# Weight loads moved from SyncE's queue to GpSimd's, one buffer of P for each step parity, and a new order, in a transformer kernel on one core

## The chip, the core and the metric

The kernel runs on one core of one Trainium2 chip. Its engines are TensorE (matmuls; PE in the profile, PEld for its weight loads), VectorE (DVE), ScalarE (ACT), GpSimd (POOL) and SyncE (SP, which issues DMAs only). SyncE, ScalarE and GpSimd can each issue DMAs, each in the order of its own queue. The metric is the device time of one launch in microseconds, lower is better.

## The reference

Two layers with the same weights run one after the other: attention over segments of 32 tokens with a recurrent memory of 8 tokens, then a gated feed-forward block (F = 4608), both with layer norm and a residual, on x of 2048 x 576.

```python
for s in range(n_seg):                       # 64 segments, one after the other
    h = concat([mem, xs], axis=1)            # 8 memory rows + 32 rows of x
    q, k, v = h @ Wq, h @ Wk, h @ Wv         # 32 heads of 128
    p = softmax(where(mask, q @ k.T * scale, -1e9))
    o = (p @ v) @ Wo
    mem = o[:, :M]                           # goes into the next segment
    outs.append(o[:, M:])
...
x = x + A(layernorm(x), mem0, ...)
x = x + (silu(h @ w1) * (h @ w3)) @ w2       # h = layernorm(x)
x = x + A(layernorm(x), mem0, ...)
x = x + (silu(h @ w1) * (h @ w3)) @ w2
```

## The kernel before

A step is one segment of layer 0 together with the segment of layer 1 that is eight behind it (LAG = 8), 72 steps in all; where both run, their 40 rows each are handled side by side. The attention weights stay in SBUF. The feed-forward weights don't fit beside them, so they are loaded again for each group of 128 tokens: in 18 pairs of 128 columns of F, 304 pair loads over the kernel. A pair needs five DMAs: two of 256 KB and two of 32 KB into W13 (its nine row chunks of w1 and w3; a 256 KB one has 512 rows of 512 bytes, a 32 KB one 64), and one of 288 KB into W2C (256 rows of 1152 bytes). W13 and W2C have two buffers each. The profile lists W13 as W.

The softmax of a step runs in four groups of eight heads (NG = 4). VectorE adds the mask and takes the maximum, ScalarE the exponential, VectorE the sum, and multiplies P into PB in the columns that the next matmul needs (`sm_pb`: the columns differ between steps of even and odd parity, `role(t)`). A DMA transposition on SyncE's queue (`ptd`, 224 of them) brings PB to PTS, or TensorE transposes it (`ptr`) where one layer runs alone. PB has two buffers, used by even and odd groups. Since a step writes other columns than the one before, the first two groups of each step wait for a memset of their buffer, which is GpSimd's work (`pb_zero`, 142 of them).

The order of all work comes from a planner. `make_nodes` (line 236 on) makes a node for each piece of work, with an engine, an assumed duration and the slots of buffers that it takes and frees. `plan` then takes TensorE's pieces in the order of the string ORDER, one letter a piece, and puts the work of the other engines into their queues as their assumed durations let it start. An assumed duration is no measurement; it only decides the order in a queue. ORDER is FIRST (16 steps), then FOUR (4 steps) eleven times, then LAST. The letters that matter here:

- Q, q: q and k (full rows, then the last 64 rows of the contraction in row mode); S: scores; T: transposition of P on TensorE; P: P times V; O, o: the product with Wo
- V, v, X, x, G, g: v
- F, f: the two halves of the product with w1 and w3 (full rows, then the last 64 in row mode); W, w: the product with w2, for layer 0 and 1
- m, a, b, p, n: transpositions for mem0, layer norms and residuals

TensorE runs in several array modes (full, col, row, c32, oct, quad), and `plan` keeps to one mode as long as the pieces allow it.

Layer norm (`ln_nodes`) is a chain over engines: statistics on VectorE, the power -1/2 on GpSimd (`ln_pow`, 64 of them), normalising into XN on VectorE, transposition on TensorE.

SyncE's queue holds, in one order, the loads of attention weights at the start, all feed-forward loads (1520 DMAs for the pair loads), the transpositions of P, the XN loads of x and at the end the weights of the last group. GpSimd's queue holds the memsets of PB, the powers, 16 loads of x into XR, and the stores. Eight semaphores are used in turn by the DMAs of each kind of queue, so a DMA also waits until the one eight before it has landed.

Of the kernel before, what the change touches and what calls it, by code (L numbers as in the profile page):

```python
# [13 lines left out]
P = 128  # L14
R64 = 64
D = 576
# [183 lines left out]
def ewh(*ns):  # L200
# [5 lines left out]
    "maqqQqQSqTQQQSqQqqSQTQqSXxVvPPTTOOPoPOooOoQqqqqQQSQVvSqqQQQTQSqqXTSPOPTPOOTooPoxOoQQqqqqQSQvVqSQqQQQSqqTPSTOPoOT"  # L206
    "PTOPooOoaQqqQQSQqqVvSqQQQqqqTSQPxTSOPXOToToPPOOooQqqqpQQSVvqqQQnQSFfqqQTQSPfqFSOTFPfWoTOPFTOPoofOoFfqqQQWSFQQqqf"
    "vVqQSTFqfQWQQSqfqFPFTSXfPWTOPOxoTFoPOOffooFVqqvQQWQSQqqfFQqqfFSQTWSPQqfqFQFSTOfPWoTOPFTOPfaOoooFfqqQQvqqSQQWSfVF"
    "qQqQWQTQPqSqTOPbSOxxXTXTPooPOOooQpQQqqqqQSnQSFfqFfQvqVSfFWQqqQfPSFPOOooFfPWOFPofOoFQqqfqQWQSqqqQQQSFSGfgqQQqgfFP"
    "GSWPGfggfFFGOPoOOPWOoooFFffqqQQWSqqQQFvSqfVqQQfFSWqQQqfPPSFFOOPWoOffFPoaoOoWQqqqqQQbSQQQqqSGSgqQQqgPGSOPGggGoPOO"  # L210
    "PooOoQqqqppQQQqvVSSnnQFfqqQQQfqqSFFSPfPwOOWoFPoffFOwPWOooFqqffQQwFWQQqqFSSFffqqQQQQqqwWSSgfGFPGgggGPGOoPOOPWOooo"
    "wFqfqqQQQQSffqqFFSQQwvqVWSFQqqffFQWPwSFffPOPOOowooWFPFOoafQQqqqWSQqqqQQQSwSbQqQgqGSggGPGPOGoPgOPOOooo"
)
FOUR = (
    "QqqqppQvVSQQnnQFqfqFSfqqQQFfqQSWPwPSFffOOowFPWoOPFOooFqfqfQQwQQqqgSWGSFqqfQQQPwQSWFqffqFSGgggGPGPOOwooOPWOooFFqq"
    "ffQQQQSwVvqqfFSQQqqWPFSFfqqfQQwOSWPFFoffPOOWPwOoooFfqqQQqqaSQQqWSQQqqqQQSbwSggGGPGPOggoGPOPOOooo"
)
LAST = (
    "QqqppQQSQqqqvVSQQnqqnQSFPqffQOoSPFOFPwWOFPfooOofQQQqqqfFSwWQQFfqqfFSwWqqQQSGqffgFQFPGgWSwPFggfGOOPoGowPOOooFvfqq"
    "VQQQQSWqqFSFqqffQQQQqqSPwWSFfPOOoWwFffPFPOOooowQWQfqqqFSFfqqQQQWSqqqQQSQbvVVSPwXvxPOPOoOPooOoQQppVqqqQQSqvqnQSnQ"  # L220
    "qffFFQTSqqQTPwFfSPWTOOPFffTFooOPWwOooFffqvVQWFQQqqqQSwSQQfqqFSTFfqqQQWTPwSPFOTOffoPTFoPOOWoowxvXVqqQQFSQqfqqQQSF"
    "QQqqqfQTwPSTSWOPFOffTFPToWoPOwOooFqqfvQQQSQqqfVwWSFFfQqqQTWqSPQQqTOSPbOxooTXPTwPOOooQQpqqqQSqQVvnSqqQQqQSQFfqTFP"
    "STfOPoTOwPTFPOOooofVvqqQQQqqSQQSFfqqFQQSTwqqQTFPffSPOTOwxXooPTFPOOffooFQQqqqqQSQFSfvVqqQQQTqqSQwTPfSOFPFTOwTooPf"
    "POfOooFvVQQqwQqqqSQqqQSQfFTSqQqQfPTSPOOooFTTPPfOOoopwfFFnFwffFFwffFFwwffFfFwFfFwffFfFwFfFwffFFwffFFwffFw"
# [11 lines left out]
def make_nodes(em, nseg, pools, o=Opt, dma_bw=230e3, load_bw=400e3):  # L236
# [125 lines left out]
    def step(t):  # L362
# [17 lines left out]
        zdep = [pts_of[t - 1, k] for k in (NG - 2, NG - 1)] if t else []  # L380
        for g in range(NG):
# [88 lines left out]
    def job(j):  # L470
# [36 lines left out]
        for at, pp in enumerate([npp - 1] + list(range(npp - 1)) if last else range(split, npp)):  # L507
# [33 lines left out]
            for (bi, g) in ents:  # L541
# [3 lines left out]
                if last and at == npp - 1:  # L545
                    xn = Slot("xn")
                    for h in (0, 1):
                        e_ = node("DVE", dve(288), em.fin_add(g, h, xr[g], xn, b[h]), deps=[d], prio=prio + o.w2, acq=[xn], rel=[b[h]], name="W2a")
                        node("SWD", 1.0, em.store_half(g, h, xn), deps=[e_], prio=s0 + LAG - 4.2, lat=2.0, name="store")
# [21 lines left out]
    def x_res(g):  # L571

        xr_ld[g] = node("SWD", 1.0, em.load_x(g, xr[g]), deps=reads_ht[4 * g + 1][:1], prio=4 * g + 1.5, acq=[xr[g]], name="ldx", lat=4.0)
# [30 lines left out]
class Emitter:  # L604
# [122 lines left out]
    def load_w13(self, pr, w13):  # L727
        def f(n):
            fa = pr * 2 * P
            W = self.T.W13[:, w13.i]  # L730
            for kind, wd in ((0, self.a.w1), (1, self.a.w3)):
                self.dma(W[:, 4 * kind:4 * kind + 4], wd[0:4 * P, fa:fa + 2 * P].rearrange("(c p) f -> p c f", p=P))
            for kind, wd in ((0, self.a.w1), (1, self.a.w3)):
                self.dma(W[kind * R64:(kind + 1) * R64, 8], wd[4 * P:D, fa:fa + 2 * P])
        return f

    def load_w2(self, pr, w2):
        fa = pr * 2 * P
        return lambda n: self.dma(self.T.W2C[:, w2.i], self.a.w2[fa:fa + 2 * P, :].rearrange("(b p) d -> p b d", p=P))
# [306 lines left out]
    def pb_zero(self, pb):  # L1046
        return lambda n: self.ch("POOL", self.nc.gpsimd.memset(self.pbt(pb), 0.0))  # L1047
# [345 lines left out]
```

## Time and profile before

| | us |
|---|---|
| median of 3 runs | 2644.6 |
| lowest, highest | 2642.23, 2646.21 |
| profiled execution, whole time | 2638.71 |
| its span, first to last instruction | 2636.9 |

The profile is one execution. Its page gives for each engine the busy time; a matmul's end is modelled, so gaps shorter than about a matmul's own time (0.2 us) don't show as idle. A row such as "1058.00 0.45 PE ... x8" in an order of time has the start in us from the span's start, the time from the first start to the last end, and how many instructions were merged; "[1.86 <-ACT HT L630]" is the idle time before it and what ended it. "busy us, mean ns" stand in the groups; "572/572/722" is the shortest, median and longest duration in ns. L627, L630 and L633 are the helpers for TensorE, ScalarE and VectorE, L636 and L642 those for DMAs of SyncE and GpSimd, L1047 is the memset of PB, L1050 the transposition.

### The profile page before, as it was taken

How to read it: one execution, taken by the hardware profiler on the slowest of the kernel's cores; microseconds unless marked ns; L12 is line 12 of the kernel's file. 1: busy time of each engine (PE TensorE's matmuls, PEld its weight loads, DVE VectorE, ACT ScalarE, POOL GpSimd, SP SyncE). 2: the span in 40 equal slices, each digit the busy share in tenths (PEclk: the TensorE clock that was granted, in tenths of full speed). 3: DMA queues.
4: the chain of work that ended last, by engine and by line, in shares of the span. 5: the costliest groups of instructions: out<-in, count | busy, mean ns of one | idle time of the engine just before them, and what ended most of it. 6: DMA issues, size and time to landing. Idle time of an engine off the chain costs nothing.

```text
span 2636.9 us, 134690 instructions
## 1 busy us (share of the span) xinstructions
PE 2574.1 (98%) x60031; PEld 2222.3 (84%) x60031; DVE 2004.5 (76%) x5137; ACT 1264.2 (48%) x3745; POOL 196.7 (7%) x253
## 2 busy tenths in 40 slices
PE   5999999999999999999999999999999999999998
PEld 4788888889888888888888888888888888888886
DVE  4787777887778678777877777787777777777876
ACT  2655553444445454444545444454545445454552
POOL 1100000000000010000001001000100001010000
PEclk9999999999999999999999999999999999999999
DMA  9065755575464656546454654655465464545357
GB/s 324 4 174 135 190 104 147 130 148 139 126 147 115 139 127 155 136 131 151 113 140 116 159 140 128 155 110 139 114 156 143 132 159 94 139 122 146 106 156 247
DMA packets 683207, 371.56 MB, mean 141 GB/s; under 512 B 233753, under 2 KB 672801, under 8 KB 681985
## 3 DMA queue, kind: packets, MB, share of 16 engines
q1 hardware_dynamic: 678944, 355.00, 53.2%
q8 instruction: 469, 7.68, 1.2%
q0 software_dynamic: 3024, 6.93, 0.9%
q10 hardware_dynamic: 656, 1.02, 0.2%
q14 instruction: 114, 0.93, 0.1%
HBM read 306.72 MB, written 2.36 MB: 117 GB/s over the span
## 4 chain that ended last, share of the span: by engine, by line
PE 91%; DVE 4%; DMA 3%; issue 1%; ACT 1%; ACTq 0%; DVEq 0%; SPq 0%
PE bank L627 91%; DMA PTS<-PB 2%; DVE HTT L633 1%; DVE PB L633 1%; DVE STAT L633 1%; DMA WV<-in_A_Wv_dram 0%; DVE SME L633 0%; DMA W<-in_A_Wk_dram 0%; DVE V L633 0%; DVE QKT L633 0%; DMA W2C<-in_B_w_dram 0%; DVE XR L633 0%; ACT HTT L630 0%; ACT HT L630 0%; DVE LNS L633 0%
## 5 line engine op out<-in xcount | busy, mean ns | idle before, releaser
L627 PEld LDWEIGHTS <-W 128*128 128x128 bf16 (+2 forms) x32920 | 1261.8, 101 | 119.8 <-issue 67.8
L627 PE MATMUL bank<-HT,W 128*128 128x80 bf16 (+3 forms) x23040 | 795.2, 197 | 21.3 <-ACT HT L630 8.2
L627 PE MATMUL bank<-XTB,W 128*64 128x256 bf16 (+5 forms) x9880 | 658.4, 264 | 2.1 <-issue 1.3
L630 ACT ACTIVATE QKT<-bank 128x256 bf16<-128x256 f32 (+4 forms) x1676 | 385.1, 309 | 302.9 <-PE bank L627 296.5
L627 PE MATMUL bank<-OT,WO 128*128 128x80 bf16 (+3 forms) x11520 | 411.6, 198 | 2.5 <-issue 1.9
L627 PEld LDWEIGHTS <-WO 128*128 128x128 bf16 (+1 forms) x11520 | 383.2, 102 | 29.9 <-issue 16.3
L630 ACT ACTIVATE V<-bank 64x512 bf16<-64x512 f32 (+1 forms) x603 | 338.0, 584 | 137.4 <-PE bank L627 131.4
L627 PE MATMUL bank<-WV,HT 128*32 128x512 bf16 (+4 forms) x3576 | 363.5, 384 | 0.3 <-issue 0.2
L627 PE MATMUL bank<-W2C,HTT 128*64 128x288 bf16 (+1 forms) x3440 | 323.8, 287 | 0.5 <-DMA W2C<-in_B_w_dram 0.5
L630 ACT ACTIVATE HTT<-bank 128x512 bf16<-128x512 f32 (+1 forms) x322 | 172.6, 551 | 300.1 <-PE bank L627 299.1
L633 DVE TENSOR_REDUCE STAT<-SME 104x8 f32<-104x320 f32 (+1 forms) x576 | 274.9, 477 | 28.2 <-ACT SME L630 21.2
L633 DVE TENSOR_TENSOR PB<-SME,STAT 40x128 bf16<-40x128 f32 (+4 forms) x912 | 274.8, 335 | 9.3 <-DMA PTS<-PB 0.5
L627 PEld LDWEIGHTS <-HT 128*32 128x32 bf16 (+4 forms) x3576 | 149.2, 99 | 147.7 <-issue 37.8
L633 DVE SCALAR_TENSOR_TENSOR HTT<-HTT,bank 128x512 bf16<-128x512 bf16 (+1 forms) x322 | 201.0, 624 | 94.4 <-ACT HTT L630 91.6
L627 PEld LDWEIGHTS <-HTT 128*64 128x64 bf16 (+1 forms) x3512 | 233.1, 106 | 31.2 <-DVE HTT L633 4.1
L1047 POOL MEMSET PB<- 128x1024 bf16 x142 | 135.0, 952 | 1657.0 <-DMA PTS<-PB 1114.3
L633 DVE SCALAR_TENSOR_TENSOR XR<-bank,XR 128x288 f32<-128x288 f32 x574 | 240.0, 447 | 20.3 <-PE bank L627 17.2
L630 ACT ACTIVATE OT<-bank 128x320 bf16<-128x320 f32 (+1 forms) x383 | 144.4, 404 | 214.5 <-PE bank L627 185.3
L630 ACT ACTIVATE SME<-SME 104x320 f32<-104x320 f32 (+1 forms) x288 | 135.5, 470 | 194.3 <-DVE SME L633 192.4
L633 DVE TENSOR_TENSOR HTT<-HTT,bank 128x512 bf16<-128x512 bf16 (+1 forms) x322 | 203.3, 631 | 28.5 <-PE bank L627 1.4
L633 DVE CAST V<-bank 64x512 bf16<-64x512 f32 (+1 forms) x261 | 178.9, 686 | 40.1 <-PE bank L627 34.9
L633 DVE TENSOR_TENSOR SME<-bank,maskb 104x320 f32<-104x320 f32 (+1 forms) x288 | 138.5, 482 | 53.8 <-PE bank L627 50.1
(59 smaller groups left out, 1383.5 us busy)
## 6 DMA issues: line engine op xcount, KB each, us to landing
W<-in_B_w_dram SPq DMA_DIRECT2D x608, 256.0 KB, 3.6
W2C<-in_B_w_dram SPq DMA_DIRECT2D x304, 288.0 KB, 3.4
W<-in_B_w_dram SPq DMA_DIRECT2D x608, 32.0 KB, 3.4
W<-in_B_w_dram SPq DMA_DIRECT2D x8, 1024.0 KB, 12.6
W<-in_A_Wq_dram SPq DMA_DIRECT2D x9, 512.0 KB, 9.9
WO<-in_A_Wo_dram SPq DMA_DIRECT2D x4, 1152.0 KB, 19.1
XR<-in_A_x_dram POOLq DMA_DIRECT2D x16, 288.0 KB, 3.1
WV<-in_B_w_dram SPq DMA_DIRECT2D x4, 1152.0 KB, 7.5
```

What stands on the lines that cost most here:

```text
L627: self.ch("PE", self.nc.tensor.matmul(out, lhsT=lhsT, rhs=rhs, start=start, stop=stop, skip_group_check=True, **k))
L630: self.ch("ACT", self.nc.scalar.activation(*a, **k))
L633: self.ch("DVE", getattr(self.nc.vector, fn_)(*a, **k))
L1047: return lambda n: self.ch("POOL", self.nc.gpsimd.memset(self.pbt(pb), 0.0))
```

## The change

Three things are changed together. All pair loads (W13, W2C) go to GpSimd's queue, and the planner has new assumed durations for that queue. PB's buffer is chosen by the parity of the step instead of by that of the group, so a buffer always has the same columns written, and it is cleared only where the kernel goes from one layer to two or back: four memsets in all, on VectorE. And the strings of ORDER are new.

```diff
 FOUR = (
-    "QqqqppQvVSQQnnQFqfqFSfqqQQFfqqQSWPwPSFffOOowFPWoOPFOooFqfqfQQwQQqqgSWGSFqqfQQQPwQSWFqffqFSGgggGPGPOOwooOPWOooFFqq"
-    "ffQQQQSwVvqqfFSQQqqWPFSFfqqfQQwOSWPFFoffPOOWPwOoooFfqqQQqqaSQQqWSQQqqqQQSbwSggGGPGPOggoGPOPOOooo"
+    "QqqqppQVvSQQnnQqfFSFqqfQQQSqqfFwPWSOFffPFoPOOWwPFOoooFfqqQQQQqqSWwGSFfgqqQQwPQQSWFqfqfFGSgggGPGOPOwoOPWOooFoFqq"
+    "ffQQQQSwvVfqqFSQQqqWPFSFqffqQQWOSwPoFFPffOOWPwOoooFqfqQQqqaSQWQQqSQqqqQQSbwSGggGPGPOggGPoOOPooOo"
 )
...
-        zdep = [pts_of[t - 1, k] for k in (NG - 2, NG - 1)] if t else []
...
-            pb = Slot(f"pb{g % 2}")
-            if g < 2 and t:
-                zero = [node("POOL", 0.95, em.pb_zero(pb), deps=zdep[g:g + 1], prio=pf, acq=[pb], name="pbz")]
+            pb = Slot(f"pb{e}")
+            if g == 0 and t > 1 and both(t) != both(t - 2):
+                zero = [node("DVE", 0.65, em.pb_zero(pb), deps=[pts_of[t - 2, NG - 1]], prio=pf - 2.0, acq=[pb], name="pbz")]
...
-            node("SWD", 1.0, em.store(g, xn), deps=[c], prio=s0 + LAG - 4.2, rel=[xn], lat=3.0, name="store")
+            node("POOL", 0.6, em.store(g, xn), deps=[c], prio=s0 + LAG - 4.2, rel=[xn], lat=3.0, name="store")
...
-                    ld = [node("DMA", kb(1152, 256) / dma_bw, em.load_w13(pr_, w13), prio=prio - 1, acq=[w13], lat=2.5, name="W13")]
-                    lds.append(node("DMA", kb(256, 576) / dma_bw, em.load_w2(pr_, w2), prio=prio - 0.99, acq=[w2], lat=2.4, name="W2l"))
+                    ld = [node("POOL", 2.25, em.load_w13(pr_, w13), prio=prio - 1, acq=[w13], lat=3.0, name="W13")]
+                    lds.append(node("POOL", 0.75, em.load_w2(pr_, w2), prio=prio - 0.99, acq=[w2], lat=2.8, name="W2l"))
...
             for kind, wd in ((0, self.a.w1), (1, self.a.w3)):
-                self.dma(W[:, 4 * kind:4 * kind + 4], wd[0:4 * P, fa:fa + 2 * P].rearrange("(c p) f -> p c f", p=P))
+                self.swdma(W[:, 4 * kind:4 * kind + 4], wd[0:4 * P, fa:fa + 2 * P].rearrange("(c p) f -> p c f", p=P))
             for kind, wd in ((0, self.a.w1), (1, self.a.w3)):
-                self.dma(W[kind * R64:(kind + 1) * R64, 8], wd[4 * P:D, fa:fa + 2 * P])
+                self.swdma(W[kind * R64:(kind + 1) * R64, 8], wd[4 * P:D, fa:fa + 2 * P])
...
-        return lambda n: self.dma(self.T.W2C[:, w2.i], self.a.w2[fa:fa + 2 * P, :].rearrange("(b p) d -> p b d", p=P))
+        return lambda n: self.swdma(self.T.W2C[:, w2.i], self.a.w2[fa:fa + 2 * P, :].rearrange("(b p) d -> p b d", p=P))
...
     def pb_zero(self, pb):
-        return lambda n: self.ch("POOL", self.nc.gpsimd.memset(self.pbt(pb), 0.0))
+        return lambda n: self.v("memset", self.pbt(pb), 0.0)
```

FIRST and LAST are new in the same way. The other lines that the diff touches give loads of XR and the last stores the same new assumed durations; the DMAs themselves stay where they were. In the changed program GpSimd's queue begins, after its constants, with the ten DMAs of the first two pairs, then the power of the first layer norm; SyncE's has after the start-up weights only the XN loads, the transpositions and the last group's weights.

More of the change, by code (lines that the diff above doesn't have):

```diff
@@ L205 @@
 FIRST = (
[L206 to L210, printed above, removed]
@@ L213 @@
+    "qfFQTWqqSPQQTOPSbOxXTXPTxooPOOooQpQqqqqQSQnQQfqSFFvqfVSQFfqqQWPfSFPOFOfWPooFOPfoOoFQfqqqQQSqqqQQWQgfSFGSfqQWFPQq"
+    "gGgSFPGffgFGOPOoWPOOoooFFqqffQQWSqqQQFvSqfVQQqfFSWqQQqfPPSFOOWPoofFOFoPfaOoWQQqqqqQSQQbQSqqGSggqGQQqPPSOGGgOPgoO"
+    "ooPOoQqqppQQQSqqvVnSnQQFfqqqQQPfqSFFSPfWOOwoFffPFOWPwOooFoFffqqQQWwQQSfqqFSFfqqQWQQQqqSwSfggGFPGGPOwggGPoOPOOooo"
+    "FfqqQQQWSfqqFQQQSwFvqqfVWSFQffqqFQWaPSPwOOFffooFPwPOOWooFfqqQQqqWSQqqQQSwQbQQqqSGSggGPGPOGggOPoOPooOo"
 )
 FOUR = (
-    "QqqqppQvVSQQnnQFqfqFSfqqQQFfqQSWPwPSFffOOowFPWoOPFOooFqfqfQQwQQqqgSWGSFqqfQQQPwQSWFqffqFSGgggGPGPOOwooOPWOooFFqq"
@@ L221 @@
[L221 to L224, printed above, removed]
+    "QqqppQQSQqqqvVSQQqqnnQfSFPfqQOSoFPFOPWwOFPfooOofQQQfqqqFSQWwQFfqqfFSGWwqgfQFSqQQPFgfqGSWwOPoFggfGGPOPOOooowWvVfq"
@@ new lines @@
+    "qFQQQQqqSFSFqqffQQQQqqSwPWSFPfOOooFPWwffFPOOowoWQQFqqfFSfqqQQqWSvQQqqQSVQbqPVPSwOXvOPoxoOPoOoQQppvqqVqqQSQQqSnnQ"
+    "qqfFFTSQQPqfTOfPSFOwWTFTPooffPFOOWwooFvqfqVQQFSQWQqqqfQwSTQqqfQSFPqfFTQPWTwSPOFOffFToOWPwOxoooXVvqqQQFQqqfSQQSqq"
+    "QFqfqQwTQSPTSWPOFOffTFToPowOPWOooFqfqvQQQSQqfqVwWSFFfqqQQTWqSQPQqTOSPbOxooTXPTwPOOooQQpqqqQSqQvVnSQqQqTFSQqfqQFP"
+    "STOfPoTOwPTFPOOooofVvqqQQQqqSQFSQqqfqQQFSTwPQqffTFSPOOTwXxoPTFoPOOffooFQQqqqqQQSFfSVvQQqqqQqSTQwTPSFFfPOOTwToPof"
+    "POOooFfqvVqQQQQSqqwfqqQSFQQSTqqQfTSPPOOoofTFPTFPOOoowpfFnwFffFFwffFFwwfFffFwFfFwffFfFwFffFwFfFwffFFwffFw"
@@ L548, in job @@
                         e_ = node("DVE", dve(288), em.fin_add(g, h, xr[g], xn, b[h]), deps=[d], prio=prio + o.w2, acq=[xn], rel=[b[h]], name="W2a")
-                        node("SWD", 1.0, em.store_half(g, h, xn), deps=[e_], prio=s0 + LAG - 4.2, lat=2.0, name="store")
+                        node("POOL", 0.6, em.store_half(g, h, xn), deps=[e_], prio=s0 + LAG - 4.2, lat=2.0, name="store")
                     return
@@ L571, in x_res @@
     def x_res(g):
-        xr_ld[g] = node("SWD", 1.0, em.load_x(g, xr[g]), deps=reads_ht[4 * g + 1][:1], prio=4 * g + 1.5, acq=[xr[g]], name="ldx", lat=4.0)
+        xr_ld[g] = node("POOL", 0.6, em.load_x(g, xr[g]), deps=reads_ht[4 * g + 1][:1], prio=4 * g + 1.5, acq=[xr[g]], name="ldx", lat=4.0)
     x_in(0)
```

8 lines of the change are left out of this document (4 added, 4 removed).

## The prediction

> **What bounds the kernel now.** I read the head of the page, then the busy times by stage, then TensorE's own waits, and last the order of time at the start and in one repeated stretch.
>
> ```profile
> span 2636.9 us, 134690 instructions
> ```
>
> ```profile
> core 0: us, PE busy (x) PEld busy (x) DVE busy (x) ACT busy (x) POOL busy (x), PEclk, DMA share, GB/s
> 0.00:60.00 60.00, 30.72 (x727) 23.27 (x729) 28.07 (x68) 15.15 (x39) 8.20 (x20) 0.94 1.00 350
> 60.00:640.00 580.00, 567.35 (x14296) 487.44 (x14293) 449.16 (x1189) 291.94 (x866) 43.93 (x54) 0.99 0.54 129
> 974.43:2196.62 1222.19, 1217.70 (x27266) 1061.25 (x27264) 936.10 (x2385) 590.74 (x1769) 89.60 (x112) 1.00 0.55 135
> 2196.62:2636.90 440.28, 424.82 (x10299) 360.97 (x10295) 333.70 (x840) 201.80 (x574) 30.55 (x37) 1.00 0.54 148
> ```
>
> These are busy times by stage. The first 60 us are loading (DMA share 1.00, 350 GB/s) and TensorE idles 29.3 us of them. From 60 to 640 it idles 12.7 us and after 2196.62 another 15.5 us. In between, in eight of the eleven repetitions of FOUR (from one of its XR loads to the eighth after it, 1222.19/8 = 152.8 us each), it idles 4.5 us in all, 0.6 us a repetition. So TensorE is the bound, and visible waits after the start come to some 33 us, 1.2% of the span. That is the most that a change of waits could bring, apart from gaps too short to show; what it can lose has no such limit.
>
> ```profile
> PE bank L627 <- ACT HT L630: 8.2, 20, 1.9
> PE bank L627 <- DMA W<-in_A_Wk_dram: 6.4, 4, 3.2
> PE bank L627 <- DMA PTS<-PB: 5.0, 11, 1.4
> PE bank L627 <- DMA W2C<-in_B_w_dram: 0.5, 1, 0.5
> ```
>
> This is the view of TensorE's waits (total, times, longest). The transpositions of P, which the change frees from SyncE's loads, cost it 5.0 us in all. For the feed-forward weights it waited 0.5 us, once: today they are in time.
>
> **What is taken away.** POOL loses the 142 clearings of PB. They lay on an engine that was mostly idle.
>
> ```profile
> L1047 POOL MEMSET PB<- x142: 951/951/970, 52.9 to 2559.4; 128x1024 bf16 x142
> L642 POOL DMA_DIRECT2D XR<-in_A_x_dram x16: 572/572/722, 54.7 to 2348.2; - x16
> ```
>
> 142 x 0.951 = 135 us of POOL, of which VectorE or TensorE waited for none: worth 0. Four clearings come to VectorE in their place, each about one such memset, under 1 us: 4 us on an engine with 936.10 of 1222.19 busy, hidden by its idle 23%. Without that cover they would cost 4 us at most.
>
> **The start.** 608 loads of 256 KB, 608 of 32 KB and 304 of W2C go to POOL, five for a pair of feed-forward blocks. In the new order of POOL's queue the first ten (two pairs) stand ahead of the first layer norm's power and need no buffer to come free. In the old one SyncE issued them behind every start-up weight, from 47.17 on.
>
> ```profile
> 1.38 0.84 ACTq L639 DMA_DIRECT2D XN<-in_A_x_dram  x1
> 5.57 0.30 POOL L1347 MEMSET maskb<- 8x40 bf16 x2
> 10.27 0.82 DVE L633 BATCH_NORM_STATS2 LNS<-XN 128x6 f32<-128x288 bf16 x2 [1.82 <-DMA XN<-in_A_x_dram]
> 11.68 0.56 POOL L796 TENSOR_TENSOR LNS<-LNS,mhalf 128x1 f32<-128x1 f32 x1 [5.81 <-DVE LNS L633]
> 15.34 0.66 PE L627 MATMUL bank<-HT,W 64*128 64x40 bf16 x19 [1.86 <-ACT HT L630]
> 23.37 2.44 PE L627 MATMUL bank<-HT,W 128*128 128x40 bf16 x65 [3.16 <-DMA W<-in_A_Wk_dram]
> 47.17 6.44 SPq L636 DMA_DIRECT2D W<-in_B_w_dram  x4
> ```
>
> This is the order of time. POOL is free at 5.9 us, and until 23.37 TensorE waits for the first half of Wq and Wk. Two pairs are 2 x (2 x 256 + 2 x 32 + 288) = 1728 KB, 1.77 MB, and at 350 GB/s that is 5.1 us of a bus already full. XN, small and on ACT's queue, shows that another queue's transfer is mixed with SyncE's rather than put behind it: issued at 1.38 it had landed by 10.27, long before SyncE's queue was done. So between 0 us (all served after the weights) and 5.1 us (all served ahead of them) comes on the path up to 23.37. From there the path is TensorE's own, and no later row can hide it. I take 3.5, since the ten start 6 us after the weights did and are mixed with them for the 17 us that are left. The power at 11.68 now stands behind loads nine and ten, which wait until loads one and two have landed (eight semaphores in turn). With XN's 8.9 us from issue to use that is 5.9 + 8.9 = 14.8 or more. The matmuls follow the power by 15.34 - 11.68 = 3.7 us, so a power up to 23 us is hidden by the wait for Wk, then near 27. Past that each microsecond costs one.
>
> **The turn-round of a weight buffer.** This decides the steady part. There are two buffers, so a pair's loads start when its last reader is done and have to land before the pair after next.
>
> ```profile
> W<-in_B_w_dram SPq DMA_DIRECT2D x608, 256.0 KB, 3.6
> W2C<-in_B_w_dram SPq DMA_DIRECT2D x304, 288.0 KB, 3.4
> W<-in_B_w_dram SPq DMA_DIRECT2D x608, 32.0 KB, 3.4
> XR<-in_A_x_dram POOLq DMA_DIRECT2D x16, 288.0 KB, 3.1
> PTS<-PB SPq DMA_TRANSPOSE x224, 3.3
> ```
>
> ```profile
> 1058.00 0.45 PE L627 MATMUL bank<-PTS,V 128*128 128x80 bf16 x8
> 1058.29 1.15 PE L627 MATMUL bank<-W2C,HTT 128*128 128x288 bf16 x8
> 1059.27 1.72 PE L627 MATMUL bank<-OT,WO 128*128 128x80 bf16 x48
> 1060.82 3.66 PE L627 MATMUL bank<-XTB,W 128*64 128x256 bf16 x64
> 1064.41 0.46 PE L627 MATMUL bank<-HT,W 64*128 64x80 bf16 x16
> 1064.71 0.60 PE L627 MATMUL bank<-XTB,W 64*128 64x256 bf16 x8
> 1069.93 0.40 PE L627 MATMUL bank<-QKT 128*64 128x40 bf16 x15
> ```
>
> ```profile
> 1062.33 6.31 SPq L636 DMA_DIRECT2D W<-in_B_w_dram  x8
> ```
>
> The first fence has the landings from issue (last column), the others the order of time on TensorE and on SyncE. SyncE took 6.31 us for eight loads, 3.2 a pair, and the last lands 3.5 later: 6.7 us, and TensorE never waited for it. On POOL the 128 rows of XR took 0.572 us to issue. A 256 KB load has 512 rows (128 partitions, four pieces each), the 32 KB one 64, W2C 256. **Bounds:** if the issue costs the same whatever the rows, a pair's four take 4 x 0.572 = 2.3 us, and with 3.5 to land 5.8. If it goes by rows (4.5 ns each), 2 x 2.29 + 2 x 0.29 = 5.2, and 8.7 in all.
>
> Against that stands the new order. Start to start the rows give P 0.29 us, W or w 0.98, O 1.0 (32 of the 48 matmuls in 1.55), F 1.8 (half of the 64 in 3.59); by their lengths f takes 0.3 (half of the 8) and S 0.4. The tightest reload in FOUR is F w P W S O F f f. Between its last reader, the first F, and its next, the last f, lie w, P, W, S, O, F and f: 5.8 us, and about 5.9 with the changes of mode. Four others lie between 6.4 and 7.0 and nine of eighteen under 8.7. Counted so, the old order has 5.3 as its tightest and five more under 6.9, and with 6.7 us it still lost nothing, since the 256 KB loads are issued first, and are free to be, before the row-mode matmuls have finished. So an allowance of about 1 us is in this count. At 5.8 nothing is late. At 8.7, less 1.0, the five tight ones and one more are short by 0.2 to 1.8, 6 us a repetition; over 2637/152.8 = 17 such stretches 100 us, and some 65 if the early and late stretches with half the load count less. I take 0.9 us for a 512-row load and 0.5 for a 64-row one, nearer to XR's row, as this is the only one for the same engine: 2.8 us a pair, shorter than SyncE's 3.2. That leaves odd hits: +3 us, ends 0 and +100.
>
> The Trainium skill, page "DMA: Bandwidth & Descriptors", section "Anatomy of one DMA", says of loads from this engine that many descriptors can be emitted before their number shows in the cost. By that the pair takes 2.3 us and this term is 0. No run here shows a load of 512 rows from POOL, so I don't lean on it.
>
> The page "SBUF — State Buffer" of the Trainium skill, section "SBUF: two separate sides", speaks against the change: while VectorE runs an operation that uses both its ports, POOL cannot write descriptors. The trace has POOL's 142 memsets at 951 to 970 ns beside a VectorE 77% busy, unstretched, so I take 0; by the rule, VectorE's normalisations of XN below (27.5 us, 1.0% of the span) would hold some 16 of the 1520 issues by up to 0.57 us each, 9 us of POOL's time at most, and the sum would be at most 2 us more, since about a fifth of the reloads are tight.
>
> ```profile
> L633 DVE TENSOR_SCALAR XN<-XR,LNS 128x576 bf16<-128x576 f32 x48 | 27.5, 573 | 1.3 <-POOL LNS L796 0.9
> ```
>
> **SyncE's queue.** Only 224 transpositions and 15 XN loads are left on it, so no transposition waits behind a load that itself waits for TensorE. Of TensorE's 5.0 us I give back 3; the ends are 0 and 5.0.
>
> **PB by parity.** The four groups of a step now share one buffer, so group g+1's multiplications wait until g's transposition has landed, and behind them on VectorE's queue wait whatever evacuations follow.
>
> ```profile
> 1006.20 1.11 DVE L633 TENSOR_TENSOR PB<-SME,STAT 40x128 bf16<-40x128 f32 x4
> 1007.35 1.57 SPq L1050 DMA_TRANSPOSE PTS<-PB  x1
> 1010.80 1.11 DVE L633 TENSOR_TENSOR PB<-SME,STAT 40x128 bf16<-40x128 f32 x4
> ```
>
> Two close groups are 4.6 us apart. The first needs 1.15 us to its transposition and 3.3 to land, 4.45. The closest pair of S in FOUR is as close in the new order as in the old. Margin 0.15 us: cost 0, and if a landing takes 4 us, 0.6 us of VectorE, which its idle time hides; bound +3 us over all.
>
> **The order.** The same 3725 pieces of TensorE work stand in a new order, and TensorE changes between its array modes 1291 times instead of 1270 (66 to 68 in FOUR, 301 and 301 before it, 242 to 241 after it).
>
> ```profile
> 1064.41 0.62 PEld L627 LDWEIGHTS <-W 64*128 64x128 bf16 x24 [0.20 <-issue]
> ```
>
> A weight load after such a change sat idle 0.20 us, some of it under the matmuls before. 21 x 0 to 0.20 = 0 to 4.2, I take 2.1. What the order does to the 28 us of idle time in the early and late stretches can't be read: 0, with 8 us either way.
>
> **Sum:** +3.5 (start) + 3 (late weights) + 2.1 (modes) - 3 (transpositions) + 0 = +5.6 us. The profiled execution took 2638.7 us, its span 2636.9 and 1.8 around it; it would become 2644.3. The median of the three runs shown is 2644.6, 5.9 above the profiled one, so the forecast for the median is 2650.
>
> **Rivals.** (1) *Faster by the softmax chain.* With SyncE's queue empty a transposition starts as soon as PB is written. PV, WO and the memory columns of HT follow it sooner, so the waits for PTS (5.0) go and with them those for HT (8.2), mostly in the early and late stretches: 2644.6 + 3.5 + 2.1 - 13.2 = 2637. It decides once more than 10.9 us come back. For it: SyncE's loads did stand ahead of transpositions, and 33 us of waits could be had. Against it: in the repeated part only 4.5 of 1222.19 us are idle, and HT waits for ACT. Chance 0.24. (2) *Slower by late weights.* POOL's issue goes by rows. Place: f and F in FOUR, waiting for W. It decides once a pair's four issues pass about 3.4 us, 1.3 us for 512 rows; at 2.29 it is +65 to +100, 2712 to 2747; between the point where it decides and there, 2680. For it: XR is the only row and has a quarter of the rows. Against: POOL's power, a single element a partition, takes 0.56 us, so a fixed part fills nearly all of 0.572. Chance 0.20. (3) *POOL's queue order.* The 64 powers now stand behind loads that wait for TensorE. If a buffer comes free later than the order assumes, the layer norm behind it is late, TensorE's transposition of XN waits, and each miss costs up to one pair's 2.8 us; on a tenth of the 64, 18 us: 2668. Against it: both releases come from the same TensorE order. Chance 0.06. The forecast has the rest, 0.50, its own range 2641 to 2664.
>
> **How the numbers follow.** Under 0.2% (5.3 us; about what a measurement of this kernel tells from none) counts as no change: 2639.3 to 2649.9. The forecast's 0.50 lies on both sides of the upper bound: 0.24 same, 0.25 slower, 0.01 faster. With rivals 2 and 3 slower has 0.51, with rival 1 faster 0.25. The range goes from 2631, with a tenth below it, to 2700, with a tenth above.
>
> **What would show it.** Start: TensorE's long run of 65 matmuls begins at 26 to 28.5 instead of 23.37. Weights: a row of TensorE waiting for W from POOL stays under 5 us in all, and the issue of a 256 KB load under 1.3 us; above that rival 2 holds. The waits for PTS fall under 2.5 us. The repetition of FOUR is 152.5 to 153.5 us. POOL's time for loads is about 304 x (2.8 + 0.65) = 1050 us. I am wrong if the start doesn't shift, if FOUR grows past 154 us, or if it shrinks below 152.

## The result and the profile after

| | before | after |
|---|---|---|
| median of 4 runs each, us | 2643.41 | 2770.36 |
| lowest, highest | 2640.14, 2646.21 | 2767.86, 2771.39 |
| ratio, 95% interval | | 1.0479 [1.0461, 1.0497] |
| span of the profiled execution | 2636.9 | 2769.2 |
| TensorE busy | 2574.1 | 2615.1 |
| idle (span less busy) | 62.8 | 154.1 |
| mean granted clock | 0.996 | 0.986 |

The change made the kernel 4.8% slower, outside the predicted range of 2631 to 2700. Of the 132.3 us by which the span grew, 91.3 are idle time of TensorE. The granted clock takes another part: 2769.2 x 0.014 = 38.8 us against 2636.9 x 0.004 = 10.5, so up to 28. What is left, 13 us, is longer busy time. Its causes weren't taken apart; the new order alone adds 8.8 of such time (e3, below).

First the busy times by stage, cut near those of before (columns as there):

```profile
core 0: us, PE busy (x) PEld busy (x) DVE busy (x) ACT busy (x) POOL busy (x), PEclk, DMA share, GB/s
0.00:62.00 62.00, 30.05 (x528) 18.06 (x529) 25.93 (x62) 12.15 (x30) 12.96 (x28) 0.89 0.96 344
62.00:660.00 598.00, 564.82 (x14054) 483.05 (x14052) 436.11 (x1164) 289.14 (x862) 232.37 (x352) 0.98 0.47 120
1020.12:2300.00 1279.88, 1232.01 (x27362) 1071.76 (x27359) 934.63 (x2377) 587.80 (x1762) 508.04 (x768) 0.99 0.53 129
2300.00:2769.20 469.20, 437.77 (x10270) 368.63 (x10268) 344.02 (x865) 204.36 (x575) 175.28 (x264) 0.97 0.49 140
```

The loss is spread over all these stages, with some 5 us at the start (see there, below). Eight repetitions of FOUR took about 1280 us, 160 each instead of 152.8, and they idle 47.9 us where they idled 4.5.

Now TensorE's waits after the change, and one of VectorE's (total, times, longest):

```profile
PE bank L626 <- DMA PTS<-PB: 61.0, 37, 4.9
PE bank L626 <- DVE XN L632: 19.5, 2, 17.8
PE bank L626 <- DMA W<-in_B_w_dram: 6.2, 6, 2.2
PE bank L626 <- DMA W2C<-in_B_w_dram: 4.5, 5, 2.0
DVE PB L632 <- DMA PTS<-PB: 95.4, 56, 4.6
```

The transpositions of P, 5.0 us before, cost 61.0. The late weights, which I thought the danger, cost 10.7 together. The 17.8 for XN stands at the very start, where TensorE would wait for the attention weights anyway. VectorE waits 95.4 us for a transposition to free the single buffer of PB.

The landings from the issue, and POOL's issue costs from its groups (busy us, mean ns; idle before and what ended it):

```profile
W<-in_B_w_dram POOLq DMA_DIRECT2D x608, 256.0 KB, 4.0
W2C<-in_B_w_dram POOLq DMA_DIRECT2D x304, 288.0 KB, 3.7
PTS<-PB SPq DMA_TRANSPOSE x224, 4.1
```

```profile
L641 POOL DMA_DIRECT2D W<-in_B_w_dram x1216 | 788.1, 654 | 604.8 <-PE bank L626 579.4 <-issue 12.9 <-DMA W<-in_B_w_dram 5.4
L641 POOL DMA_DIRECT2D W2C<-in_B_w_dram x304 | 223.1, 735 | 493.0 <-PE bank L626 486.0 <-issue 4.6 <-DMA W<-in_B_w_dram 1.9
```

A transposition lands 4.1 us after its issue instead of 3.3. Issuing stayed cheap, 654 ns on the mean.

One stall shows the mechanism. These are the order of time in the changed kernel on POOL, SyncE, VectorE and TensorE around 1860 us, and the busy times in the windows of 3.4 us around the stall:

```profile
1853.80 2.60 POOL L641 DMA_DIRECT2D W<-in_B_w_dram  x4 [3.80 <-PE bank L626]
1856.39 1.47 POOL L641 DMA_DIRECT2D W2C<-in_B_w_dram  x2
1859.29 4.76 POOL L641 DMA_DIRECT2D W<-in_B_w_dram  x7 [1.43 <-PE bank L626]
...
1855.97 1.12 DVE L632 TENSOR_TENSOR PB<-SME,STAT 40x128 bf16<-40x128 f32 x4
1865.54 1.12 DVE L632 TENSOR_TENSOR PB<-SME,STAT 40x128 bf16<-40x128 f32 x4 [4.56 <-DMA PTS<-PB]
...
1861.95 0.31 PE L626 MATMUL bank<-OT,WO 128*64 128x80 bf16 x8
1865.49 0.75 PE L626 MATMUL bank<-PTS,V 128*64 128x80 bf16 x16 [3.22 <-DMA PTS<-PB]
```

```profile
1857.10 0.02 SPq L1049
1857.12 0.03 issue
1857.15 8.29 DMA PTS<-PB
1865.44 0.04 issue
```

```profile
1858.50:1861.90 3.40, 3.40 (x65) 2.90 (x64) 2.44 (x7) 1.57 (x4) 2.58 (x4) 1.00 0.97 122
1861.90:1864.94 3.04, 0.36 (x13) 0.24 (x8) 0.00 (x0) 0.42 (x1) 2.06 (x3) 1.00 1.05 154
1864.94:1868.35 3.41, 2.86 (x50) 2.77 (x51) 2.73 (x7) 0.77 (x2) 0.54 (x1) 0.50 1.01 340
1868.35:1871.76 3.41, 3.41 (x59) 3.01 (x58) 2.41 (x5) 0.00 (x0) 0.12 (x1) 1.00 0.51 86
```

PB is written by 1857.1 and SyncE, whose queue is empty, issues at once. But POOL has just put six loads on the bus and puts seven more there from 1859.29, and the transposition lands 8.3 us after its issue (the second fence is the chain of waits). TensorE stands still 3.22 us. VectorE can't write the next group into PB until then, so that group's transposition is late as well. And after the stall TensorE runs one stretch of 3.41 us at half clock.

### The profile page after: what moved, and what is told of

It is laid out like the page before. It is cut to its first block, busy times and chain, and to the rows that moved or that the text cites. A ratio compares the mean times of both kernels' runs of the same rounds, so it can differ in the third digit from the quotient of the medians.

```text
span 2769.2 us, 134269 instructions
## 1 busy us (share of the span) xinstructions
PE 2615.1 (94%) x60034; PEld 2246.5 (81%) x60034; DVE 2010.4 (73%) x5151; ACT 1262.3 (46%) x3735; POOL 1073.4 (39%) x1631
## 4 chain that ended last, share of the span: by engine, by line
PE 76%; DMA 15%; DVE 5%; issue 3%; POOL 1%; ACT 1%; DVEq 0%; SPq 0%; ACTq 0%; POOLq 0%
PE bank L626 76%; DMA PTS<-PB 12%; DVE PB L632 2%; DVE HTT L632 1%; DMA W<-in_A_Wk_dram 1%; POOL W L641 1%; DVE STAT L632 1%; DVE SME L632 1%; DMA W<-in_B_w_dram 1%; DMA W2C<-in_B_w_dram 1%; DMA XN<-in_A_x_dram 0%; DVE V L632 0%; DVE QKT L632 0%; ACT SME L629 0%; ACT HT L629 0%
## 5 line engine op out<-in xcount | busy, mean ns | idle before, releaser
L641 POOL DMA_DIRECT2D W<-in_B_w_dram x1216 | 788.1, 654 | 604.8 <-PE bank L626 579.4
L626 PE MATMUL bank<-XTB,W 128*64 128x256 bf16 (+4 forms) x9976 | 664.3, 265 | 10.4 <-DMA W<-in_B_w_dram 6.2
L629 ACT ACTIVATE QKT<-bank 128x64 bf16<-128x64 f32 (+4 forms) x1664 | 382.5, 311 | 281.9 <-PE bank L626 258.4
L626 PE MATMUL bank<-OT,WO 128*128 128x80 bf16 (+3 forms) x11520 | 423.4, 200 | 4.1 <-issue 2.2
L626 PEld LDWEIGHTS <-WO 128*128 128x128 bf16 (+1 forms) x11520 | 392.8, 103 | 30.8 <-issue 14.6
L641 POOL DMA_DIRECT2D W2C<-in_B_w_dram x304 | 223.1, 735 | 493.0 <-PE bank L626 486.0
L629 ACT ACTIVATE V<-bank 32x512 bf16<-32x512 f32 (+1 forms) x587 | 330.7, 585 | 135.1 <-PE bank L626 125.5
L629 ACT ACTIVATE OT<-bank 128x320 bf16<-128x320 f32 (+1 forms) x403 | 151.4, 405 | 343.5 <-PE bank L626 319.4
L632 DVE TENSOR_REDUCE STAT<-SME 104x8 f32<-104x320 f32 (+1 forms) x576 | 274.5, 477 | 25.1 <-ACT SME L629 18.6
L795 POOL TENSOR_TENSOR LNS<-LNS,mhalf 128x1 f32<-128x1 f32 x64 | 40.1, 627 | 484.9 <-DVE LNS L632 475.8
```

Source lines behind the costliest of these rows:

```text
L626: self.ch("PE", self.nc.tensor.matmul(out, lhsT=lhsT, rhs=rhs, start=start, stop=stop, skip_group_check=True, **k))
L629: self.ch("ACT", self.nc.scalar.activation(*a, **k))
L632: self.ch("DVE", getattr(self.nc.vector, fn_)(*a, **k))
L641: self.ch("POOL", self.nc.gpsimd.dma_start(out=out, in_=in_))
L795: self.ch("POOL", self.nc.gpsimd.tensor_tensor(L[:, 15:16], L[:, 14:15], self.T.mhalf[:], op=ALU.pow))
```

## The experiments

All ratios are to the old kernel on the same chip. The first four take the change apart: "loads" is the move to GpSimd's queue, "parity" the buffer of PB by parity with its clearing, "order" the strings. Each keeps the hunks named in the table and no others; these are the lines that make the first two, the third is the strings alone.

```diff
-                self.dma(W[:, 4 * kind:4 * kind + 4], wd[0:4 * P, fa:fa + 2 * P].rearrange("(c p) f -> p c f", p=P))
+                self.swdma(W[:, 4 * kind:4 * kind + 4], wd[0:4 * P, fa:fa + 2 * P].rearrange("(c p) f -> p c f", p=P))
```

```diff
-            pb = Slot(f"pb{g % 2}")
+            pb = Slot(f"pb{e}")
```

Three theories were stated: A, the single buffer of PB; B, longer landings beside GpSimd's loads; C, the new order.

> The kernel before with the pair loads alone moved to GpSimd (two buffers of PB by group, cleared by GpSimd, old order). Theory A (one PB buffer within a step is the cause): TensorE's wait for PTS stays under 15 us, time 2640 to 2665. Theory B (loads from GpSimd make the transpositions land later, 4.1 instead of 3.3 us, and that is the cause): PTS waits over 40 us, time 2700 to 2770. Theory C (the new order is the cause): 2640 to 2660.

> The kernel before with PB by parity alone (one buffer within a step, four clearings on VectorE; loads on SyncE, old order). Theory A: VectorE's PB waits for PTS 60 to 100 us in all and TensorE loses 60 to 110 us, time 2705 to 2755. Theory B: landings stay at 3.3 us, time 2640 to 2660. Theory C: 2640 to 2660.

> The kernel before with the new strings of ORDER alone. Theory A and B: 2640 to 2665, PTS waits under 15 us. Theory C: 2700 to 2770, with TensorE's idle time spread over many releasers.

> The changed kernel with PB as before (two buffers by group, 142 clearings on GpSimd between the loads). Theory A: most of the 127 us comes back, 2645 to 2680. Theory B: 2740 to 2780, landings still 4.1 us. Theory C: 2740 to 2780.

| run | hunks kept | us, before, ratio | PTS waits of TensorE | PTS landing |
|---|---|---|---|---|
| e1 | loads | 2712.66, 2632.48, 1.0305 [1.0274, 1.0336] | 54.9 | 4.2 |
| e2 | parity | 2725.03, 2632.48, 1.0347 [1.0310, 1.0384] | 58.6 | 3.0 |
| e3 | order | 2658.85, 2632.48, 1.0094 [1.0071, 1.0118] | 8.4 | 3.2 |
| e4 | loads, order | 2707.37, 2632.48, 1.0270 [1.0246, 1.0293] | 34.8 | 4.1 |

Each of the three costs by itself: +80, +92 and +26 us. The loads cost what B said (e1), the parity what A said (e2). C, the order as the main cause, gave 2700 to 2770 for e3 and falls, though the order does cost something. e4 lies outside the ranges of all three theories, since each had put the loss on one cause, and the three together cost less than their sum. Loads and parity both end in waits for PTS, but with parity alone the landings are as short as ever.

A missed one thing in e2: VectorE's own waits for PTS are 18.4 us (below), not 60 to 100. There the planner, which knows of the single buffer, puts other work of VectorE first: a multiplication into PB starts 0.84 us after the sums that it needs, on the mean, where it took 0.44 in before.

**Four buffers, and no loads (e5, e6).** The next kernels take away one cause each. e5 keeps the parity but gives each parity two buffers:

```diff
-            pb = Slot(f"pb{e}")
+            pb = Slot(f"pb{2 * e + g % 2}")
...
-    T.PB = sp.tile([P, 2, GH, P], BF, name="PB")
+    T.PB = sp.tile([P, 4, GH, P], BF, name="PB")
-    T.WO = wp.tile([P, H, D], BF, name="WO")
+    T.WO = wp.tile([P, H - 4, D], BF, name="WO")
```

e6 is the changed kernel with `load_w13` and `load_w2` issuing nothing after the second pair:

```diff
     def load_w13(self, pr, w13):
+        self.n13 = getattr(self, "n13", 0) + 1
+        skip = self.n13 > 2
         def f(n):
+            if skip:
+                return
```

> The old kernel with PB by parity of steps as in the change, but two buffers for each parity, used by even and odd groups, so four in all; cleared eight times on VectorE. To make room in SBUF the WO tile holds 28 heads and the last four heads use those of the four before (a part of the computation that is changed; the matmuls are the same in number and size). PB by parity with one buffer a parity took 2725.0 against 2632.5 (+92.5). Theory A (the single buffer puts each group's transposition, with its landing, in front of the next group's multiplication): the loss goes; 2625 to 2645, TensorE's waits for PTS under 12 us in all, VectorE's for PTS under 2. Rival A2 (it isn't the number of buffers: the clearing on VectorE, the columns by parity or the planner's other order of VectorE's work costs it): above 2690, waits for PTS above 40.

> The changed kernel without the pair loads after the first two pairs: 302 of the 304 pair loads are left out, so all feed-forward products but those of the last group use the weights of the first two pairs; all else, the order of all work too, is as in the change. Theory B (the loads' bytes beside a transposition in flight make it land late): every transposition lands in about 2.6 us, TensorE's waits for PTS fall from 61 to under 10 us, the granted clock is back at 0.993 or more, and the time is 2640 to 2670, near that of the new order alone (2658.9). With 1.15 + 2.6 = 3.75 us the single buffer then fits under the 4.6 us between close groups. Rival B2 (the transpositions are late for what precedes them: the planned order on VectorE, ScalarE and GpSimd, or the single buffer by itself): waits for PTS stay above 30 us and the time above 2700.

e5: 2632.34 against 2633.02, 1.0000 [0.9991, 1.0010]. e6: 2647.0, 1.0050 [1.0032, 1.0068], clock 0.993, transpositions landing in 2.6 us in the median. These are the waits for PTS in e2, then in e5, then in e6:

```profile
PE bank L626 <- DMA PTS<-PB: 58.6, 33, 4.2
DVE PB L632 <- DMA PTS<-PB: 18.4, 24, 4.0
```

```profile
PE bank L626 <- DMA PTS<-PB: 5.8, 8, 1.7
DVE PB L632 <- DMA PTS<-PB: 2.2, 1, 2.2
```

```profile
PE bank L626 <- DMA PTS<-PB: 4.4, 7, 1.3
DVE PB L632 <- DMA PTS<-PB: 9.0, 14, 1.5
```

With two buffers a parity the whole loss of the parity is gone, so it was the number of buffers and nothing else in that hunk. Without the loads the single buffer is nearly harmless. In e6 and in the change alike, nine tenths of the transpositions are issued within 0.07 us of PB being written, so between these two it is the landings that differ. Both theories hold: the chain multiplication, transposition, next multiplication through one buffer is too long once the landings are longer than bare.

**The order, the small loads (e7, e8).** e7 is the change without the new strings, e8 the old kernel with a part of the loads moved:

```diff
-                self.dma(W[kind * R64:(kind + 1) * R64, 8], wd[4 * P:D, fa:fa + 2 * P])
+                self.swdma(W[kind * R64:(kind + 1) * R64, 8], wd[4 * P:D, fa:fa + 2 * P])
...
-        return lambda n: self.dma(self.T.W2C[:, w2.i], ...
+        return lambda n: self.swdma(self.T.W2C[:, w2.i], ...
```

> The changed kernel with the strings of ORDER as they were before: loads on GpSimd's queue and PB by parity. Theory C (the new order is part of the loss, +26 us as when made alone): about 2735 to 2750 on the scale of 2632 for the old kernel. Rival C2 (the new order was made for the other two changes and wins back part of their loss, as the three losses taken alone, 80 + 92 + 26, are more than the 127 of all together): 2775 to 2810, with waits for PTS above 70 us.

> The old kernel with only the 32 KB loads and W2C (352 of a pair's 864 KB) issued by GpSimd and the 256 KB loads left on SyncE. Theory B by dose (what lies in another queue beside a transposition is mixed with it): between the old kernel and all loads on GpSimd (+80 us), about +15 to +40 us, transpositions landing in 3.3 to 3.8 us. Rival B3 (the 32 KB and W2C loads are harmless, and SyncE's shorter queue lets transpositions start sooner): -8 to +5 us, TensorE's waits for PTS at 5 us or under.

e7: 2832.43 against 2633.02, 1.0736 [1.0686, 1.0785], waits for PTS 111.8. That is what C2 said, and more of it than its 2775 to 2810. The new order alone costs 0.9%, but beside the other two parts it wins 2.6% (1.0736 to 1.0479, 68 us). e8: 2656.56, 1.0080 [1.0061, 1.0099], landings 3.7. The time is inside theory B's dose, but not by its wait: PTS cost 4.5, W2C 10.7.

**Is it the clearings (e9 to e12)?** With PB as before, 142 clearings stand in GpSimd's queue among loads that wait for TensorE. That was a rival to B (M). e9 is the four buffers of e5 with the loads on GpSimd; e10 the change without its loads hunk; e11 the change with PB by groups as before and cleared on VectorE; e12 the change with four buffers.

```diff
-                zero = [node("POOL", 0.95, em.pb_zero(pb), deps=zdep[g:g + 1], prio=pf, acq=[pb], name="pbz")]
+                zero = [node("DVE", 0.65, em.pb_zero(pb), deps=zdep[g:g + 1], prio=pf, acq=[pb], name="pbz")]
```

(e11 against e4, with `pb_zero` on VectorE as in the change.)

> The old kernel with all pair loads on GpSimd's queue as in the change and four buffers of PB (two for each parity, cleared eight times on VectorE; the WO tile holds 28 heads and the last four heads use those of the four before, which changes that part of the computation). The loads alone, with PB still cleared 142 times on GpSimd, took 2712.7 against 2632.5, with 54.9 us of waits for PTS. Theory B (those waits come from landings that are longer beside GpSimd's loads, 4.2 instead of 3.3 us in the median): 2690 to 2720, waits for PTS above 40 us. Rival M (they come from the 142 clearings, which then stand in GpSimd's queue behind loads that wait for TensorE, and hold up the multiplication into PB): 2640 to 2660, waits for PTS under 20 us, although the landings stay at 4.1 or more.

> The changed kernel with the pair loads back on SyncE's queue: PB by parity and the new order. Alone these cost 92.5 and 26.4. Theory A with the landings of SyncE's loads (3.0 to 3.3 us in the median, nine tenths under 4.4): if the new order spreads the groups of a step no better than the old, the two add, 2735 to 2755, waits for PTS 55 us or more; rival C2 (the new order gives the single buffer more time, as it gave the change as a whole 62 us back): 2665 to 2710, waits for PTS under 40 us.

> The changed kernel with PB used by even and odd groups as before, but its 142 clearings on VectorE instead of GpSimd; loads on GpSimd and the new order stay. With the clearings on GpSimd this took 2707.4 against 2632.5 (34.8 us of waits for PTS). Rival M (clearings behind loads): 2655 to 2680, waits for PTS under 15 us; VectorE has 142 x 0.49 = 70 us more to do, in its idle time. Theory B (landings): 2700 to 2730, waits for PTS above 30 us.

> The changed kernel, loads on GpSimd and the new order, with four buffers of PB instead of two, as above (the last four heads of WO are those of the four before). Theories A and M together (the chain through the single buffer in the change, the clearings in the loads alone): 2650 to 2675, that is the new order's +26 and late weights; waits for PTS under 15 us, granted clock 0.992 or more. Theory B (long landings by themselves): 2695 to 2725, near the 2707 of loads and order alone.

| run | loads on | PB | order | ratio to 2635.76 | PTS waits | PTS landing |
|---|---|---|---|---|---|---|
| e9 | GpSimd | four | old | 1.0348 [1.0323, 1.0372] | 55.0 | 4.4 |
| e10 | SyncE | one a parity | new | 1.0217 [1.0199, 1.0236] | 30.0 | 3.1 |
| e11 | GpSimd | two, VectorE clears | new | 1.0438 [1.0413, 1.0463] | 62.2 | 4.1 |
| e12 | GpSimd | four | new | 1.0359 [1.0332, 1.0385] | 45.9 | 4.2 |

M falls: without any clearing on GpSimd the loads still cost 3.5%, no less than with them (e1). e9 and e12 come out a little above the ranges of theory B, e11 above both. e10 came as its rival C2 said, in time (2693.5) and in waits. In e9, with neither clearings on GpSimd nor a single buffer, the long landings are what is left to make the waits. In e11 VectorE waits 113.0 us for PTS before it can clear a buffer or write it, where in e4 an idle engine waited for that.

**Why the landings are longer (e13 to e16).** The first idea was the amount of load bytes that GpSimd puts beside a transposition, as nothing spaces its loads. e13 is e9 with the first load behind each transposition, in the planned order, held until that has landed; e15 the same on the changed kernel; in e14 each load waits for the third one before it. The lines of e13 (`tr` is the last transposition), then of e14:

```diff
         i = self.ch("POOL", self.nc.gpsimd.dma_start(out=out, in_=in_))
+        if self.tr is not None:
+            self.tc.add_manual_dep(i.ins, self.tr.ins.name, self.sync_dep, reason="after the transposition")
+            self.tr = None
```

```diff
         i = self.ch("POOL", self.nc.gpsimd.dma_start(out=out, in_=in_))
+        if len(self.lds) >= 3:
+            self.tc.add_manual_dep(i.ins, self.lds[-3].ins.name, self.sync_dep, reason="in flight")
+        self.lds.append(i)
```

> The old kernel with the loads on GpSimd and four buffers of PB (2727.9 against 2635.8; waits for PTS 55.0, landings 4.4 us in the median), and one wait more: the first load that GpSimd issues after a transposition in the planned order waits until that transposition has landed, so no later load starts beside it (190 of the loads wait so). Theory B1 (what counts is how many bytes of loads lie beside a transposition, since GpSimd issues them as soon as TensorE frees the buffer): landings 3.3 us or less in the median, waits for PTS under 25 us, later weights cost 5 to 30, 2650 to 2695. Rival B4 (a transposition on SyncE's queue is slow whenever another queue holds loads, also those issued before it, or GpSimd's writing of descriptors slows it): landings stay at 4.0 or more and the time at 2715 or more.

> The same kernel as the one with loads on GpSimd and four buffers of PB, but each pair load waits until the third one before it has landed, so at most three are in flight (544 to 832 KB) where there were up to eight. Theory B1: the landings with over 800 KB beside them (48 of 196, 5.75 us in the median) all but go; landings 3.9 us or less in the median, waits for PTS under 40 us; but a pair's five loads then take about 5/3 x 3.6 = 6 us, near the 5.3 to 5.9 us between readers, so waits for W and W2C rise to 15 to 50 us; 2680 to 2740. Rival B4: landings 4.2 or more, waits for PTS above 50 us.

> The changed kernel with the same wait of GpSimd's loads for a transposition ahead of them in the planned order. Theories A and B1 together: the landings fall back to 3.3 us or less, and the single buffer costs what it costs beside SyncE's loads (2693.5 against 2635.8 for the change with SyncE's loads): 2680 to 2725, waits for PTS 20 to 40 us. Rival B4: 2755 or more.

e13: 2838.3, 1.0763 [1.0740, 1.0786]. e14: 2951.34, 1.1203 [1.1176, 1.1229]. e15: 2899.96, 1.1027 [1.0987, 1.1068] (before: 2633.43). Landings 4.4, 4.0, 4.4 us: theory B1 missed those that it gave in all three, and only in e14 were the waits for PTS (29.9) where it put them. The times are above its ranges, too. Rival B4 came true in e13 and e15, but missed e14, for which it gave landings of 4.2 or more and waits above 50. These are waits in e13:

```profile
PE bank L628 <- DMA W<-in_B_w_dram: 86.7, 62, 5.1
PE bank L628 <- DMA PTS<-PB: 31.1, 26, 3.1
POOL W L643 <- DMA PTS<-PB: 187.1, 40, 8.8
```

GpSimd stands 187.1 us for the transpositions, and TensorE then waits 86.7 for weights (97.0 in e14, 102.4 in e15). The hold wasn't what it was meant to be: the load bytes issued beside a transposition fell only from 322 to 213 KB on the mean, those of loads planned ahead of it but issued behind it. So the times of e13 to e15 don't tell the theories apart. They show that there is no time to hold the weights back.

So I fitted, for each run, the landings in its trace to two sums of load bytes: those in flight at the issue ("ahead") and those issued from then until 1.5 us before the landing ("behind"). A long landing also gathers more behind it, so the last column proves less than the one before.

```
run     loads on  transp. on  landings  mean KB ahead, behind  mean us  us per 100 KB ahead, behind
before  SyncE     SyncE       139       171, 176               3.49     0.00, 0.25
e3      SyncE     SyncE       197       276, 143               3.35     0.01, 0.24
e10     SyncE     SyncE       197       277, 136               3.36     0.00, 0.26
after   GpSimd    SyncE       196       376, 312               4.22     0.13, 0.27
e9      GpSimd    SyncE       196       386, 322               4.38     0.13, 0.32
e16     SyncE     ScalarE     167       243, 298               4.23     0.21, 0.21
```

Each row is one profiled execution; the trace doesn't hold all 224 landings. Of the loads' landings 574 are missing in before, 379 in e16, 191 in e3 and e10 and 2 in the other two, so the row of before is the weakest. On one queue, loads ahead cost a transposition nothing that these fits show; with GpSimd's queue beside it, 0.13 us for each 100 KB.

The sums depend on their bounds, though. Counted over a fixed stretch, the 1.5 us from the issue on, and with the instruction packets (below) as a third term, loads ahead cost 0.06 to 0.09 us for each 100 KB in the runs with one queue (before, e2, e3, e5, e10) and 0.20 to 0.28 in those with two (the change, e1, e9, e16). Loads behind cost -0.03 to 0.06 and 0.19 to 0.37. What stands is that loads ahead on another queue cost about three times as much, not that they cost nothing on the same one; and the 0.25 for loads behind on one queue doesn't stand.

e16 asks whether that is GpSimd's doing:

```diff
-        return lambda n: self.ch("SP", self.nc.sync.dma_start(out=self.T.PTS[:, pts.i], ...
+        return lambda n: self.ch("ACT", self.nc.scalar.dma_start(out=self.T.PTS[:, pts.i], ...
```

> The old kernel with only the transpositions of P moved, from SyncE's queue to ScalarE's; the loads stay on SyncE, PB has its two buffers cleared on GpSimd. Read by the landings. In the old kernel, a fit of them to the KB of loads in flight at the issue (171 on the mean) and the KB issued after it gives 0.00 us for each 100 KB ahead and 0.25 for each 100 KB behind; with loads on GpSimd 0.13 and 0.27 (376 KB ahead). Rival B4 in its general form (loads on another queue than the transposition's are mixed with it, those ahead too): 0.1 us or more for each 100 KB ahead, median landing 3.6 to 4.3 us. In its narrow form (only GpSimd's loads do this): 0.00 to 0.04, median 3.0 to 3.5. The time says less, since ScalarE's evacuations now stand behind transpositions that wait for VectorE: 2650 to 2800.

e16: 2733.09 against 2642.32, 1.0356 [1.0326, 1.0386]. Landings and TensorE's waits in it:

```profile
PTS<-PB ACTq DMA_TRANSPOSE x224, 4.2
```

```profile
PE bank L627 <- DMA PTS<-PB: 43.0, 43, 2.6
PE bank L627 <- ACT HT L630: 16.6, 30, 1.8
```

GpSimd issues no load here, and the landings are as long as in the change. Two queues are enough. ScalarE's queue isn't slow in itself: 27 of its landings, with no load and no instruction packet seen beside them, took 2.6 us in the median, as on SyncE's. The Trainium skill, page "DMA: Bandwidth & Descriptors", section "Queues, rings and completion order", says that each DMA engine takes packets from the queues that it has work for by turns. The fits agree with that, 0.13 and 0.21 against 0.00 (0.24 and 0.28 against 0.06 to 0.09 over the fixed stretch); I hadn't drawn this rule into the prediction.

**What the fits of the table leave out.** The page of every run lists a DMA queue for instructions (packets, MB, share of the 16 DMA engines' span):

```profile
q8 instruction: 469, 7.68, 1.2%
```

Such a packet has 16 KB and takes about 1 us. In e6, where no weight load stands beside a transposition, the 102 landings with no such packet under way between 0.7 and 2.5 us after the issue took 2.6 us in the median, the 94 with one 3.5, and all 33 that took over 4 us had one. With the loads on the same queue, too, nearly all landings over 4 us had one: 45 of 48 in before, 48 of 52 in e2. In the change it is 62 of 108. So the long landings that the single buffer met in e2 go mostly with instruction packets, and the second queue adds more of them. No run here takes these packets away, so this is a coincidence in time and not a tested cause.

No version was found that beats both kernels. e5 is level with the old one, and all others are slower.

## Why the prediction was wrong

- **PB by parity, "cost 0", bound +3 us: the step that failed first.** Alone it cost 92 us (e2), with four buffers nothing (e5). I set 1.15 + 3.3 = 4.45 us against 4.6 between the closest groups and called a landing of 4 us "0.6 us of VectorE, which its idle time hides". Three faults: 3.3 was a median, and in the trace of before a tenth of the 139 landings seen took about 4.6 us or more, the longest 6.0. The issue isn't always prompt either where loads stand ahead of it on SyncE's queue: in e2 a tenth of the transpositions began 1.7 us or more after PB was written. And VectorE's idle time hides nothing here, since what it waits to do is the next link of TensorE's own chain, and its queue is in order.
- **SyncE's queue, "-3": wrong in sign.** The issue did get freer (in before a tenth began 1.5 us or more after PB was written, in the change 0.07 us or more), but the landing grew from 3.3 to 4.1 us, and TensorE's waits from 5.0 to 61.0. I had used that queues mix, for XN and the ten loads at the start, and didn't apply it to the transpositions, though the loads were now on another queue than they. Worth +80 alone (e1), +92 with four buffers (e9).
- **Late weights, +3 (0 to +100): right in mechanism, too small in size.** W and W2C cost 10.7 us. The 32 KB load cost 0.54 us to issue and the 256 KB one 2 x 0.654 - 0.54 = 0.77, under my 0.9 and far from the 2.29 of rows; POOL's loads took 788.1 + 223.1 = 1011 us for my 1050. So rival 2 is out, though its 2680 to 2747 came nearer to the time. The two signs that I had given for it disagree: the wait for W alone, 6.2, is past 5, and the issue is far under 1.3.
- **Start, +3.5: about right with the old order, small with the new.** In e1, against 23.37 in before:

```profile
27.20 2.44 PE L627 MATMUL bank<-HT,W 128*128 128x40 bf16 x65 [2.83 <-DMA W<-in_A_Wk_dram]
```

  That is 3.8 us later. Rows of TensorE's order of time in the change and in e10, which has the same order but SyncE's loads:

```profile
28.16 2.19 PE L626 MATMUL bank<-HT,W 128*128 128x40 bf16 x80
```

```profile
22.93 2.06 PE L626 MATMUL bank<-HT,W 128*128 128x40 bf16 x80
```

  This one is 5.2 us later, just past the upper end of 5.1.
- **The order, +2.1 with 8 either way: too small alone, wrong in kind.** +26 us alone (e3). Against the profiled execution of before, 6 us longer than the runs beside e3, its span is 18.6 us longer: 7.0 idle, 2.8 clock and 8.8 busy. But beside the other two parts it wins 68 us (e7). Its worth depends on what the transpositions need, and can't be a term by itself.
- **Clock: no term at all.** I counted a stall at its own length. Up to 28 us of the loss are stretches at half clock behind the stalls.
- **Rival 1** needed 10.9 us back from PTS and HT; HT gave 1.5 (8.2 to 6.7). **Rival 3** doesn't show: of XN's 19.5 us all but 1.7 lie at the start.

My main tests worked. "FOUR grows past 154" came true at 160, and the PTS waits didn't fall under 2.5.

## What to carry to other kernels

A buffer that is handed through a DMA needs its count from the long landings, not from the median, and a wait on an engine's queue is only hidden if nothing behind it feeds the bound engine. Before moving bulk loads to another queue, look for small, urgent transfers that shared the old one: loads in flight ahead of them slow them about three times as much from another queue as on their own. Price a stall of 2 to 3 us of TensorE with the half clock that often follows.

## What the runs showed of the hardware

- A transposition of P lands in 2.6 us in the median when no load and no instruction packet is beside it (102 landings in e6), in 3.0 to 3.3 with the loads on its own queue (before, e2, e3, e10) and in 4.1 to 4.4 with all of them on another (the change, e1, e9, e16). Each 100 KB in flight ahead of it on another queue goes with 0.13 to 0.28 us more, on its own queue with 0.00 to 0.09.
- The granted clock can fall to 0.50 for 3.41 us after a stall. In the windows around the stall near 1862 us TensorE was busy 0.36 of 3.04 us, and the next window stood at 0.50. Not every stall does this: of the 22 idle times of TensorE over 1.9 us that the change has after its first 62 us, 15 came with such a stretch, and 7, of 2.0 to 2.6 us, didn't. The Trainium skill, page "TensorE: Matmul & The Clock Gate", part 1 on the clock gate, gives windows of 3413 ns and half rate after an idle one; the lengths agree, but here an idle time shorter than a window was enough.
- From GpSimd the issue of a DMA with 512 rows costs 0.77 us, of one with 64 rows 0.54, so little of it goes by rows.
